# Twelve unread products in front, and another order for the folds and sums of layer 0

## The chip, the cores and the metric

The kernel runs on one core of a Trainium2 chip. The metric is the time of one execution on the device in microseconds (us). Three executions of the kernel before took 771.44, 772.28 and 772.64 us; the median is 772.28.

The engines' names in the profile are PE (TensorE, the matrix products; PEld is its weight load), DVE (VectorE), ACT (ScalarE), POOL (GpSimd) and SP, whose queue issues the loads and stores here. Each runs its own instructions in program order; they wait for one another through semaphores.

## What is computed

Two layers, each a Fourier block and a linear-attention block with residual sums, on x of 2048 rows by 640 columns. Cut to its core:

```python
def _A_ref(x, dft_seq_re, dft_seq_im, dft_hid_re, dft_hid_im):
    a = jnp.einsum("bsd,ed->bse", x, dft_hid_re)
    b = jnp.einsum("bsd,ed->bse", x, dft_hid_im)
    return jnp.einsum("ts,bse->bte", dft_seq_re, a) - jnp.einsum("ts,bse->bte", dft_seq_im, b)

def _B_ref(x, wqkv, wo):                       # 32 heads of 20
    q, k, v = split_heads(x @ wqkv)
    phi = lambda t: jnp.where(t > 0, t + 1, jnp.exp(t)) + 1e-6
    kv = jnp.einsum("bhsd,bhse->bhde", phi(k), v)
    z = phi(k).sum(over s)
    o = (phi(q) @ kv) / (phi(q) . z + 1e-6)
    return merge_heads(o) @ wo

for layer in range(2):
    x = x + _A_ref(_layernorm(x), ...)
    x = x + _B_ref(_layernorm(x), wqkv, wo)
```

## The kernel before

x stands in 16 tiles of 128 rows by 640 columns, x0 to x15. The host permutes rows and columns so that the symmetries of the real Fourier transform become plain sums and differences of tiles. Float32 operands of most products are split into a high and a low part, so that one product of the reference is three on TensorE; the low parts come from subtractions on VectorE (L122, `split`) after a copy on ScalarE (L121).

**The start of layer 0.** The tiles form four quads of four. Per tile there is a fold (the letter `f`, L665, or L663 where it also returns a row sum), a difference (`d`, L670), two columns that have no mirror (`k`, L780), and statistics (`s`: on VectorE L743 to L745, on ScalarE L739 and L740, or a fold's sum with ScalarE's L735). Per quad there are the scales (`r`, `scales2`: L756, L758, L759 on VectorE or POOL, then a power, L760, always on POOL) and the shifts (`o`, L768 and L769, on POOL here). Then follow the normalization (`n`, `norm2`, L776 and L777 on ScalarE), two sums (`a` and `b`, L807; for quad 0 `a` is L803 to L805), and the quad's odd part (`c`, L679, with one more row copied by L681 for quad 0). The odd parts are the moving operands of the first products on TensorE, 20 products of 128 by 512 against the class-2 cosines `cw` (L1010). Their sums are split (`u`, L938 and L939) and feed the hidden transforms (L956). `t`, `z`, `p`, `m` give the even parts, `x` loads a class of cosines, `w` and `v` split the hidden matrices, `R` and `V` swap parts of rows and tiles between the odd parts, and `g` prepares three rows (L1151 and L1152).

The string START lists all of this in the order in which the engines get it: each entry has a letter, the number of a tile or a quad in hexadecimal, and the engine (`v` VectorE, `a` ScalarE, `p` POOL, `d` a load on SP's queue). `Fold.script` (L619) walks through it. There is already a letter for products that nobody reads:

```python
            if kind == "h":
                pw = k.psum()
                for _ in range(int(c or 1)):
                    nc.tensor.matmul(pw[:, :512], k.ident, self.X[i][:, :512], start=True, stop=True)
                continue
```

It opens a PSUM buffer and multiplies the identity with 512 columns of a tile of x.

**The loads.** SP's queue loads the tiles of x in order; LOADS says behind which tiles the four class-2 loads (256 KB each) stand.

**The rest of layer 0.** The Fourier outputs follow a plan (PLANS): `o` an output pair (mixed by L984 to L988 and L995, L996), `s` a sequence product of a class and a column block (L915, L920) whose result is split into `u` by `keep` (L121, L122; class 0 has two columns more, which a second, small split takes), `w` and `q` the weights' splits, `b` and `t` the start of attention with the first statistics (L94 to L96). There are four PSUM buffers of 1024 columns, used in turn, so a sequence product waits until the split of the fourth before it has read its buffer. Keys, values and a Gram matrix follow (L155, L241), then the combine of the heads (L393, L403, L439 and splits of 120 by 120 and 120 by 640), then the outputs: per tile L439 on POOL, a sum over each head's denominators (L455), a reciprocal (L456, L457), a division (L459, L465), transposes on TensorE (L127), a split and products with the weights (L155). Outside the start, a scheduler decides the order of instructions by priorities; AHEAD moves single pieces of work forward or back in it by an offset, keyed by part, name and index (part 0 is layer 0 up to its combine).

**Check and saves.** While keys and values run, VectorE reduces pieces of the constants (L1085, a check of the symmetries); STEPS says at which tiles in the two halves of that loop, in both layers. SAVES says where layer 0 stores its split weights for layer 1. The check's verdict (L1107 to L1119) comes with the first outputs of layer 1.

```python
                if check is not None and n in STEPS[1]:
                    check.step(n != STEPS[1][-1])
```

Of the kernel before, what the change touches and what calls it, by code (L numbers as in the profile page):

```python
# [39 lines left out]
RESID = ((4, 4), (0, 3))  # L40
PLANS = ('o11 s02 s01 s12 s00 s10 s11 b w q o03t', 's00 o12 s10 s11 b s01 s02 s12 o01t w q')
COL = (0, 1, 3, 2)
WLOWS = ((4, 0), (1, 1))
PAUSES = (4, 10, 11, 12, 13, 14)
AHEAD = {'2keep00': -60, '2out10': -600, '1q13': 60, '2keep01': 600, '2keep02': 5, '0kv0': 60, '2out02': -20, '1q14': 60, '2out01': 20, '0kv2': -600, '0m1': -5, '0kv5': 60, '1weigh15': -20, '1res13': 5, '2m1': -20, '0first': -5, '2out12': -200, '2weigh1': 5, '2first': 60, '0m3': 20, '2out13': -200, '0hi01': 200, '0query5': -5, '0chunks9': -20, '0lo10': 60, '0begin': 200, '0norm1': -600, '0lo03': -600, '0key8': -200, '0lo02': -20, '0hi02': 600, '0key1': -20, '0chunks6': -600, '0query7': 20, '0norm10': -600, '0key10': 60, '0stats6': 20, '0w0': 60, '0stats5': -200, '0lo13': -60, '0out02': 600, '0key3': -60, '0norm9': -200, '0pks8': -600, '0stats2': 600, '0hi11': 600, '0lo11': 60, '0pks3': 600, '0query1': 60, '0query2': 5, '0query0': 600, '0normed3': -20, '0out00': -600, '0query10': 200, '0hi03': -60, '0query4': -5, '0out11': -600, '0chunks3': 5, '0normed7': -200, '0out12': -600, '0pks5': -5, '0normed8': -60, '0pks0': 600, '0key2': 600, '0norm3': 60, '0chunks0': 200, '0stats7': 600, '0keep10': 60, '0keep02': 20, '0keep00': -20, '0lo00': 600, '0keep01': -60, '0out03': 600, '0key4': 200, '0chunks4': 60, '0lo12': -200, '0stats9': 200, '0chunks7': -5, '0chunks2': 5, '0norm14': 20, '0wo2': -600, '0gram7': -20, '0stats13': -200, '0pks7': -20, '0normed2': 20, '0stats15': 60, '0gram6': 20, '0pks9': -600, '0stats11': -60, '0norm6': 600, '0key9': 600, '0kv4': -200, '0chunks5': -60, '0chunks13': 60, '0wo0': -20, '0normed13': 20, '0key13': -5, '0normed14': -600, '0pks6': -600, '0chunks15': -600, '0normed0': 200, '0chunks12': -600, '0acc': 20, '0query13': 5, '0chunks11': 20, '0chunks14': -5, '0gram0': 60, '0weigh1': -20, '0pks10': 20, '0key7': 60, '0gram15': 200, '0norm2': -5, '0chunks10': 200, '0pks13': 60, '0query8': 600, '0gram12': -200, '0query15': 5, '0pks14': 5, '0pks2': -5, '0norm11': -600, '0normed10': 60, '0chunks1': -600, '0pks4': 20, '0pks12': 200, '0gram4': -20, '0wo5': -20, '0gram2': -600, '0normed1': 600, '0gram11': 600, '0stats4': -200, '0gram10': -600, '0norm5': -20, '0stats12': -5}


class K:
# [111 lines left out]
class Attention:  # L160
# [92 lines left out]
    def keys_values(self, check=None, keep=1, saves=()):  # L253
# [619 lines left out]
class Fourier:  # L873
# [249 lines left out]
def fast_path(k, ctx, x, wqkv, wo, mask, sign, cls, cex, hid, ckc, ckh, out):  # L1123
# [259 lines left out]
```

## Time and profile before

| | us |
|---|---|
| median of three executions (lowest, highest) | 772.28 (771.44, 772.64) |
| the profiled execution | 772.54 |
| its span in the profile | 770.7 |
| TensorE busy | 734.4 |
| VectorE busy | 571.4 |
| ScalarE busy | 342.8 |
| POOL busy | 251.0 |
| first product on TensorE | 23.05 |

The span runs from the first to the last instruction in the profile. A line of a timeline has the start, the duration, the engine, the line of the kernel, the operation, what it writes and reads, the size and the number of instructions, and in brackets how long the engine had been idle and what ended that. A line of a table of windows has the window and its length, then for PE, PEld, DVE, ACT and POOL the busy time and in brackets the number of instructions, the granted TensorE clock as a share, the DMA engines' busy share, and GB/s. A product of float32 operands leaves two records; a product's records overlap, so that the spacing of their starts is shorter than their duration.

### The profile page before, as it was taken

The numbers are of one execution on the slowest core, as the hardware profiler recorded it, in microseconds if no ns is written. First come the engines' busy times: TensorE is split into PE (matmuls) and PEld (weight loads), VectorE is DVE, ScalarE is ACT, GpSimd is POOL, SyncE is SP. The second block draws the span as 40 slices with busy tenths as digits, with TensorE's granted clock in tenths as the row PEclk, the third lists the DMA queues.
The fourth block names the chain that finished last, engine by engine and source line by source line (L and its number), as shares of the span: only waits on it lengthen the run. The fifth ranks groups of instructions, "written<-read, shape, count | busy, mean of one in ns | idle before, by whom it ended". The sixth has DMA issues, their size and how long they took to land.

```text
span 770.7 us, 12819 instructions
## 1 busy us (share of the span) xinstructions
PE 734.4 (95%) x4862; PEld 703.1 (91%) x4862; DVE 571.4 (74%) x1147; ACT 342.8 (44%) x649; POOL 251.0 (33%) x266
## 2 busy tenths in 40 slices
PE   0899999999999999999999999999999999989996
PEld 0388999999999999899977999999999999979996
DVE  7999865658737697888975794566873799599982
ACT  7744444454334534455682334445433454331110
POOL 5347932220011112467763581111002111143300
PEclk9999999999999999999999999999999999999999
DMA  9222515332716443500052220424231443101112
GB/s 325 92 89 86 160 29 189 114 108 78 250 64 182 147 153 93 155 1 1 19 188 69 69 91 1 148 76 146 58 111 55 146 148 121 52 12 70 69 70 72
DMA packets 35101, 79.13 MB, mean 103 GB/s; under 512 B 4276, under 2 KB 6071, under 8 KB 35031
## 3 DMA queue, kind: packets, MB, share of 16 engines
q1 hardware_dynamic: 35031, 78.23, 32.1%
q8 instruction: 40, 0.66, 0.4%
q14 instruction: 30, 0.25, 0.1%
HBM read 66.01 MB, written 11.80 MB: 101 GB/s over the span
## 4 chain that ended last, share of the span: by engine, by line
PE 74%; DVE 15%; ACT 5%; DMA 2%; issue 1%; POOL 1%; SPq 0%; DVEq 0%; ACTq 0%; POOLq 0%
PE ps L155 46%; PE ps L241 14%; PE ps L956 5%; PE ps L127 4%; PE ps L1010 2%; DVE w L122 2%; PE ps L915 2%; DVE t L122 2%; DMA x<-in_x 2%; DVE t L459 1%; DVE ps L455 1%; DVE x L481 1%; PE ps L393 1%; ACT ab L776 1%; ACT ab L777 1%
## 5 line engine op out<-in xcount | busy, mean ns | idle before, releaser
L155 PE MATMUL ps<-w,t 128*128 128x320 f32 x2880 | 439.0, 311 | 2.0 <-DVE t L122 1.2
L155 PEld LDWEIGHTS ps<-w,t 128*128 128x128 f32 x2880 | 423.1, 188 | 2.8 <-DVE t L122 1.7
L241 PE MATMUL ps<-t,t 128*128 128x256 f32 (+1 forms) x640 | 139.8, 309 | 0.0
L289 POOL TENSOR_TENSOR t<-t,s 128x640 f32<-128x640 f32 x32 | 57.7, 1802 | 222.0 <-DVE s L276 206.9
L273 ACT ACTIVATE t<-ps 128x640 f32<-128x640 f32 x64 | 45.2, 706 | 154.0 <-PE ps L155 154.0
L241 PEld LDWEIGHTS ps<-t,t 128*128 128x128 f32 x640 | 107.4, 188 | 0.0
L1085 DVE CUSTOM_DVE_ANT_0 junk<-ck,ck 128x688 bf16<-128x688 f32 (+5 forms) x138 | 100.0, 724 | 3.2 <-DMA ck<-in_ck 1.3
L241 PE MATMUL ps<-w,t 128*128 128x384 f32 (+1 forms) x320 | 98.7, 310 | 0.3 <-DVE w L122 0.3
L439 POOL TENSOR_TENSOR t<-pq,t 128x640 f32<-128x640 f32 x32 | 53.9, 1690 | 96.4 <-ACT t L362 46.4
L122 DVE TENSOR_TENSOR t<-ps,t 128x640 fp32r<-128x640 f32 (+1 forms) x66 | 53.9, 817 | 40.5 <-ACT t L121 39.7
L121 ACT CAST t<-ps 128x640 fp32r<-128x640 f32 (+1 forms) x66 | 45.8, 694 | 82.7 <-PE ps L127 78.1
L276 DVE SCALAR_TENSOR_TENSOR pq<-t,pq 128x640 f32<-128x640 f32 x32 | 26.8, 837 | 56.5 <-ACT t L275 56.5
L241 PEld LDWEIGHTS ps<-w,t 128*128 128x128 f32 x320 | 60.2, 188 | 0.7 <-DVE w L122 0.5
L1010 PE MATMUL ps<-cw,ab 128*128 128x512 f32 x80 | 37.4, 624 | 23.0 <-DMA cw<-in_se 23.0
L1010 PEld LDWEIGHTS ps<-cw,ab 128*128 128x128 f32 x80 | 15.6, 200 | 42.2 <-ACT ab L777 23.0
L956 PE MATMUL ps<-t,u 128*128 128x322 f32 x306 | 48.0, 315 | 0.2 <-DVE u L939 0.2
L275 ACT ACTIVATE t<-t 128x640 f32<-128x640 f32 x64 | 48.0, 750 | 0.0
L956 PEld LDWEIGHTS ps<-t,u 128*128 128x128 f32 x306 | 45.9, 189 | 1.7 <-ACT u L938 0.8
L127 PE MATMUL ps<-ident,t 128*128 128x128 f32 x320 | 46.1, 275 | 0.1
L122 DVE TENSOR_TENSOR t<-t,t 128x640 fp32r<-128x640 f32 x32 | 26.3, 823 | 20.4 <-ACT t L121 20.3
L115 DVE TENSOR_SCALAR t<-x,kept 128x640 f32<-128x640 f32 x58 | 40.6, 701 | 0.8 <-PE ps L241 0.8
L121 ACT CAST t<-t 128x640 fp32r<-128x640 f32 x32 | 23.3, 729 | 38.7 <-DVE t L115 38.7
(171 smaller groups left out, 885.6 us busy)
## 6 DMA issues: line engine op xcount, KB each, us to landing
ck<-in_ck SPq DMA_DIRECT2D x48, 346.0 KB
ck<-in_ck SPq DMA_DIRECT2D x48, 344.0 KB
save<-w SPq DMA_DIRECT2D x20, 320.0 KB
w<-save SPq DMA_DIRECT2D x20, 320.0 KB
x<-in_x SPq DMA_DIRECT2D x16, 320.0 KB
out<-x SPq DMA_DIRECT2D x15, 320.0 KB
raw<-in_wqkv SPq DMA_DIRECT2D x10, 320.0 KB
s<-in_wqkv SPq DMA_DIRECT2D x10, 320.0 KB
```

Of the source, the lines that this page charges most:

```text
L121: self.nc.scalar.copy(hi, src)
L122: self.engine(pool).tensor_tensor(lo, src, hi.bitcast(F32), op=ALU.subtract)
L127: self.nc.tensor.transpose(tp[:, 128 * c : 128 * c + 128], src[:, 128 * c : 128 * c + 128], self.ident)
L155: nc.tensor.matmul(pu[:m, 512 * h : 512 * h + HD], s, w[:, HD * h : HD * h + HD], start=first, stop=last)
L241: nc.tensor.matmul(self.place(G, c, part), x[:, 128 * c : 128 * c + 128], p[:, f : f + n], start=start and i == 0, stop=stop and i == 2, s ...
L273: nc.scalar.activation(h2(e), halves(pu), AF.Relu, scale=-1.0)
L275: nc.scalar.activation(e, e, AF.Exp, scale=-1.0)
L289: nc.gpsimd.tensor_tensor(pksum, pksum, pk, op=ALU.add)
L439: k.nc.gpsimd.tensor_tensor(t1, self.PQ[self.order2[n]], self.zb, op=ALU.mult)
L956: self.k.nc.tensor.matmul(po[:, o : o + 322], s[:, f : f + 128], w[:, x, :], start=start, stop=stop)
L1010: self.k.nc.tensor.matmul(self.sum(j), T.out["o", q][:, 128 * j : 128 * j + 128], self.C[2, g], start=n == 0, stop=n == 3)
L1085: i = nc.vector.tensor_tensor_reduce(k.junk[:, : a.shape[1]], b, a, 1.0, 0.0, op0, op1, o)
```

## The change

START gets an entry `h712e` right after its first one: twelve products of the identity with x7, read by nobody, ahead of everything else on TensorE. The rest of START is a new order: quad 0's scale is now computed on POOL whole (`r0p` for `r0v o0p`), POOL takes other folds (`d4p`, `f3p`, `d7p`, `fap` in place of `d4p`, `d3p`, `f3p`, `d7p`, `f8p`, `fap`), and VectorE's and ScalarE's entries stand in another sequence. LOADS puts the first class-2 load behind x12 and the other three behind x14 (before: x9, x13, x15, x15). PLANS of layer 0 moves the sequence product s11 ahead of s00 and s10, and the split of the first weights behind the others. STEPS and SAVES have other tiles, and AHEAD other keys and offsets for part 0; those of the other parts are the same.

```diff
-STEPS = ((2, 3, 5, 6, 7, 10, 11, 12, 13), (0, 3, 7, 10, 14))
-SAVES = ((1, 2, 3, 5, 11), (4, 5, 6, 7, 8))
+STEPS = ((1, 3, 4, 5, 6, 10, 11, 12, 13), (1, 4, 8, 9, 10))
+SAVES = ((1, 2, 4, 8, 9), (0, 1, 5, 6, 8))
-START = 'O0p d0v s0a k1a f0v k2a d1v f1v k0a f2v s1q x00d d2v d4p s3v s2v s4a d3p k6a r0v s5a f6v s6q k3a k5a o0p f3p f7v d7p s7a f8p
...
+START = 'O0p h712e d0v s0a k1a d4p f0v d1v k2a f1v d2v f2v k0a s1q s2v s4a s3v d3v f6v x10d k6a s5a r0p k3a f3p f7v s7a k5a n2a s6q d7p fap f8v
...
-LOADS = (9, 13, 15, 15)
+LOADS = (12, 14, 14, 14)
-PLANS = ('o11 s02 s01 s12 s00 s10 s11 b w q o03t', 's00 o12 s10 s11 b s01 s02 s12 o01t w q')
+PLANS = ('o11 s02 s01 s12 s11 s00 s10 w q b o03t', 's00 o12 s10 s11 b s01 s02 s12 o01t w q')
...
```

On TensorE the twelve products come first; the 20 products with the odd parts follow in the order that they had. How instructions move on VectorE is shown at the three places that the prediction speaks of (ab_8 to ab_23 are the working copies of x0 to x15; the last number of a name is that of its buffer).

First, VectorE in the start, from the folds ahead of quad 3's variances (qve_52 before, qve_53 now) to quad 2's second sum (L807 into ab_16). Before:

```order
L665 TENSOR_TENSOR ab_19_166<-x11_120 128x319
L670 TENSOR_TENSOR ab_20_167<-x12_122 128x319
L670 TENSOR_TENSOR ab_21_168<-x13_124 128x319
L665 TENSOR_TENSOR ab_17_164<-x9_114 128x319
L756 TENSOR_SCALAR qve_52_325<-qmv_42_258 128x3
L758 TENSOR_SCALAR qve_52_325<-qmv_42_258 128x1
L759 TENSOR_SCALAR qmv_42_258<-qmv_42_258 128x1
L670 TENSOR_TENSOR ab_19_166<-x11_120 128x319
L670 TENSOR_TENSOR ab_16_163<-x8_112 128x319
L807 SCALAR_TENSOR_TENSOR ab_17_164<-ab_17_164,qrs_48_277,ab_18_165 128x640
L665 TENSOR_TENSOR ab_23_170<-x15_130 128x319
L807 SCALAR_TENSOR_TENSOR ab_16_163<-ab_16_163,qrs_48_277,ab_19_166 128x640
```

Now:

```order
L670 TENSOR_TENSOR ab_20_167<-x12_120 128x319
L670 TENSOR_TENSOR ab_21_168<-x13_124 128x319
L756 TENSOR_SCALAR qve_53_335<-qmv_42_263 128x3
L758 TENSOR_SCALAR qve_53_335<-qmv_42_263 128x1
L759 TENSOR_SCALAR qmv_42_263<-qmv_42_263 128x1
L670 TENSOR_TENSOR ab_17_164<-x9_114 128x319
L670 TENSOR_TENSOR ab_16_163<-x8_112 128x319
L665 TENSOR_TENSOR ab_17_164<-x9_114 128x319
L670 TENSOR_TENSOR ab_19_166<-x11_118 128x319
L665 TENSOR_TENSOR ab_23_170<-x15_134 128x319
L807 SCALAR_TENSOR_TENSOR ab_17_164<-ab_17_164,qrs_49_291,ab_18_165 128x640
L807 SCALAR_TENSOR_TENSOR ab_16_163<-ab_16_163,qrs_49_291,ab_19_166 128x640
```

From quad 1's odd part (L679 into ab_14, row not shown) to the variances there were five folds and differences, of which four stand here, and there are three now, of which two stand here. Behind the variances five of them stand in a row ahead of the first L807, where there were two, and the two L807 follow each other.

Second, VectorE in the Fourier outputs of layer 0, from the split of the first sequence product's sums (u_119 before, u_120 now, 128x2x256) to the small split of the same product's two further columns (128x2), after which its PSUM buffer is free. Before:

```order
L122 TENSOR_TENSOR u_119_599<-ps_117_592,u_118_598 128x2x256
L96 BN_AGGR kept_195_880<-st_197_882 128x2
L94 BN_STATS st_223_1074<-x15_130 128x6
L95 BN_STATS st_223_1074<-x15_130 128x6
L95 BN_STATS st_210_977<-x12_122 128x6
L987 TENSOR_TENSOR x13_124<-x13_124,t_115_583 128x321
L122 TENSOR_TENSOR u_122_613<-ps_120_606,u_121_612 128x2x256
L94 BN_STATS st_240_1185<-x9_114 128x6
L122 TENSOR_TENSOR u_119_599<-ps_117_592,u_118_598 128x2
```

Now:

```order
L122 TENSOR_TENSOR u_120_612<-ps_118_605,u_119_611 128x2x256
L96 BN_AGGR kept_167_735<-st_169_737 128x2
L96 BN_AGGR kept_196_893<-st_198_895 128x2
L987 TENSOR_TENSOR x13_124<-x13_124,t_116_596 128x321
L95 BN_STATS st_211_990<-x12_120 128x6
L122 TENSOR_TENSOR u_123_626<-ps_121_619,u_122_625 128x2x256
L94 BN_STATS st_228_1101<-x15_134 128x6
L95 BN_STATS st_228_1101<-x15_134 128x6
L122 TENSOR_TENSOR u_120_612<-ps_118_605,u_119_611 128x2
```

One half of a tile's statistics (L94 or L95) fewer stands ahead of the small split, three in place of four, and one aggregate (L96) more. L1152, which stood among the first mixes (L984), now stands ahead of the first of them.

Third, VectorE where the outputs of layer 1 begin. Before:

```order
L457 RECIPROCAL rden_1254_7490<-den_1253_7489 128x32
L122 TENSOR_TENSOR w_1243_7448<-ps_1241_7440,w_1242_7447 120x640
L122 TENSOR_TENSOR w_1246_7461<-ps_1244_7453,w_1245_7460 120x640
L456 TENSOR_SCALAR den_1262_7570<-den_1262_7570 128x32
L459 TENSOR_TENSOR t_1250_7479<-pq_1126_6774,rden_1254_7490 128x5x120
L122 TENSOR_TENSOR w_1249_7474<-ps_1247_7466,w_1248_7473 120x640
L465 TENSOR_TENSOR t_1250_7479<-pq_1126_6774,rden_1254_7490 128x2x5x4
L122 TENSOR_TENSOR t_1259_7557<-ps_1252_7483,t_1258_7556 128x640
L457 RECIPROCAL rden_1263_7571<-den_1262_7570 128x32
L455 TENSOR_REDUCE den_1269_7622<-t_1260_7562 128x32
L1109 TENSOR_REDUCE cktop_7544<-ps_1256_7542 8x1
```

Now:

```order
L122 TENSOR_TENSOR w_1244_7461<-ps_1242_7453,w_1243_7460 120x640
L122 TENSOR_TENSOR w_1247_7474<-ps_1245_7466,w_1246_7473 120x640
L455 TENSOR_REDUCE den_1263_7583<-t_1252_7494 128x32
L456 TENSOR_SCALAR den_1254_7502<-den_1254_7502 128x32
L122 TENSOR_TENSOR w_1250_7487<-ps_1248_7479,w_1249_7486 120x640
L122 TENSOR_TENSOR t_1260_7570<-ps_1253_7496,t_1259_7569 128x640
L456 TENSOR_SCALAR den_1263_7583<-den_1263_7583 128x32
L457 RECIPROCAL rden_1255_7503<-den_1254_7502 128x32
L1109 TENSOR_REDUCE cktop_7557<-ps_1257_7555 8x1
L457 RECIPROCAL rden_1264_7584<-den_1263_7583 128x32
L459 TENSOR_TENSOR t_1251_7492<-pq_1131_6803,rden_1255_7503 128x5x120
```

The last weight split (w_1249 before, w_1250 now), the split of the first tile's transposed rows (t_1259, now t_1260) and the check's maximum (L1109) stood behind the first of these divisions (L459), and stand ahead of it now.

More of the change, by code (lines that the diff above doesn't have):

```diff
@@ L30 @@
 CUT = 10
-STEPS = ((2, 3, 5, 6, 7, 10, 11, 12, 13), (0, 3, 7, 10, 14))
-SAVES = ((1, 2, 3, 5, 11), (4, 5, 6, 7, 8))
-START = 'O0p d0v s0a k1a f0v k2a d1v f1v k0a f2v s1q x00d d2v d4p s3v s2v s4a d3p k6a r0v s5a f6v s6q k3a k5a o0p f3p f7v d7p s7a f8p s8v s9v n2a k4a sav d6v x10d dav n3a fap n0a kaa sda r1v kfa o1p sbv b0v k7a f4v r2v sev a0v sca d5v n7a c0v dfv f5v n6a a1v b1v dev c1v d9v o2p sfa fbv R0a dcv k8a ddv f9v r3v dbv k9a x01d w01a naa d8v b2v kba V0a x11d nba ffv o3p w00a a2v fev kca c2v fcv kda kea fdv nfa a3v w02a nea b3v c3v t2v v01v V1a t3v v00v t0v t1v w12a v02v u23v w10a u21v u20v u22v w11a v11v v10v u24v v12v z0v p0v p1v m1p m0v g0a'
+STEPS = ((1, 3, 4, 5, 6, 10, 11, 12, 13), (1, 4, 8, 9, 10))
+SAVES = ((1, 2, 4, 8, 9), (0, 1, 5, 6, 8))
+START = 'O0p h712e d0v s0a k1a d4p f0v d1v k2a f1v d2v f2v k0a s1q s2v s4a s3v d3v f6v x10d k6a s5a r0p k3a f3p f7v s7a k5a n2a s6q d7p fap f8v s9v n3a s8v sav sca n0a d6v sda dav d5v x00d r1v kaa k7a b0v kfa k4a sbv f4v r2v sev o1p a0v n7a dfv c0v f5v a1v n6a b1v dev c1v sfa R0a fbv dcv ddv o2p r3v d9v d8v f9v dbv k8a x01d k9a naa w01a kba nba ffv V0a b2v a2v fev x11d c2v kca o3p fcv fdv kea nfa w02a kda w00a a3v nea b3v c3v V1a v00v v01v t3v v02v t1v t0v w11a t2v u23v w10a u21v u20v u24v w12a v11v u22v v12v v10v g0a z0v p0v m0v p1v m1p'
 SECOND = 'x02d x12d x22d x32d x00d x01d x10d x11d W00d W01d W02d W10d | w00a | w01a v00v W11d | w02a v01v W12d | v02v | R0a V0a w10a | O0p sfa v10v ffv dfp kfa r3p | w11a c2v v11v w12a nfa v12v nea t2p a3v b3v c3v V1a t3p p1v m1p u20v u21v u23v u24v u22v'
@@ L44 @@
 PAUSES = (4, 10, 11, 12, 13, 14)
-AHEAD = {'2keep00': -60, '2out10': -600, '1q13': 60, '2keep01': 600, '2keep02': 5, '0kv0': 60, '2out02': -20, '1q14': 60, '2out01': 20, '0kv2': -600, '0m1': -5, '0kv5': 60, '1weigh15': -20, '1res13': 5, '2m1': -20, '0first': -5, '2out12': -200, '2weigh1': 5, '2first': 60, '0m3': 20, '2out13': -200, '0hi01': 200, '0query5': -5, '0chunks9': -20, '0lo10': 60, '0begin': 200, '0norm1': -600, '0lo03': -600, '0key8': -200, '0lo02': -20, '0hi02': 600, '0key1': -20, '0chunks6': -600, '0query7': 20, '0norm10': -600, '0key10': 60, '0stats6': 20, '0w0': 60, '0stats5': -200, '0lo13': -60, '0out02': 600, '0key3': -60, '0norm9': -200, '0pks8': -600, '0stats2': 600, '0hi11': 600, '0lo11': 60, '0pks3': 600, '0query1': 60, '0query2': 5, '0query0': 600, '0normed3': -20, '0out00': -600, '0query10': 200, '0hi03': -60, '0query4': -5, '0out11': -600, '0chunks3': 5, '0normed7': -200, '0out12': -600, '0pks5': -5, '0normed8': -60, '0pks0': 600, '0key2': 600, '0norm3': 60, '0chunks0': 200, '0stats7': 600, '0keep10': 60, '0keep02': 20, '0keep00': -20, '0lo00': 600, '0keep01': -60, '0out03': 600, '0key4': 200, '0chunks4': 60, '0lo12': -200, '0stats9': 200, '0chunks7': -5, '0chunks2': 5, '0norm14': 20, '0wo2': -600, '0gram7': -20, '0stats13': -200, '0pks7': -20, '0normed2': 20, '0stats15': 60, '0gram6': 20, '0pks9': -600, '0stats11': -60, '0norm6': 600, '0key9': 600, '0kv4': -200, '0chunks5': -60, '0chunks13': 60, '0wo0': -20, '0normed13': 20, '0key13': -5, '0normed14': -600, '0pks6': -600, '0chunks15': -600, '0normed0': 200, '0chunks12': -600, '0acc': 20, '0query13': 5, '0chunks11': 20, '0chunks14': -5, '0gram0': 60, '0weigh1': -20, '0pks10': 20, '0key7': 60, '0gram15': 200, '0norm2': -5, '0chunks10': 200, '0pks13': 60, '0query8': 600, '0gram12': -200, '0query15': 5, '0pks14': 5, '0pks2': -5, '0norm11': -600, '0normed10': 60, '0chunks1': -600, '0pks4': 20, '0pks12': 200, '0gram4': -20, '0wo5': -20, '0gram2': -600, '0normed1': 600, '0gram11': 600, '0stats4': -200, '0gram10': -600, '0norm5': -20, '0stats12': -5}
@@ new lines @@
+AHEAD = {'2keep00': -60, '2out10': -600, '1q13': 60, '2keep01': 600, '2keep02': 5, '0kv0': -5, '2out02': -20, '1q14': 60, '2out01': 20, '0kv2': 5, '0m1': -5, '0kv5': 200, '1weigh15': -20, '1res13': 5, '2m1': -20, '0first': -5, '2out12': -200, '2weigh1': 5, '2first': 60, '2out13': -200, '0hi01': 200, '0chunks9': 600, '0lo10': -200, '0lo03': -600, '0lo02': 20, '0key1': -5, '0norm10': -600, '0key10': 600, '0stats6': 20, '0w0': 60, '0lo13': -60, '0out02': 600, '0key3': 20, '0pks8': -5, '0stats2': 20, '0hi11': 200, '0lo11': 60, '0query0': -200, '0normed3': 60, '0out00': -600, '0out11': -600, '0chunks3': -600, '0out12': -600, '0pks0': 200, '0keep10': 60, '0keep02': 20, '0lo00': 600, '0keep01': -60, '0out03': 600, '0key4': -60, '0chunks4': 20, '0lo12': -60, '0chunks7': -20, '0chunks2': 5, '0gram7': -600, '0normed2': -60, '0stats15': 60, '0gram6': -200, '0kv4': -5, '0chunks5': 5, '0chunks13': 60, '0wo0': -20, '0normed13': 20, '0chunks15': -600, '0normed0': -60, '0chunks11': 60, '0gram15': 200, '0norm2': -5, '0chunks10': 200, '0gram12': 20, '0query15': 5, '0pks2': -5, '0chunks1': -600, '0wo5': 5, '0gram2': -5, '0normed1': 600, '0gram11': 600, '0gram8': -200, '0normed4': 5, '0key12': 20, '0stats3': -20, '0pks15': -20, '0stats0': -600, '0query6': -60, '0gram3': 200, '0norm12': 200, '0query3': 5, '0gram9': -20, '0gram1': 60, '0norm15': -20, '0chunks8': 200, '0weigh1': 60, '0stats8': -200, '0hi00': -5, '0pks14': 200, '0hi13': 5, '0m2': 200, '0kv1': -200, '0query13': 600, '0norm8': -200, '0norm13': 600, '0gram13': -5, '0norm5': -200, '0gram5': -60, '0out10': -20, '0pks9': -60, '0norm11': -200, '0pz2': -600, '0stats1': 20, '0norm3': -20, '0norm9': -20, '0keep00': 600, '0gram10': -200, '0normed8': -200, '0pks5': 5, '0m5': 20, '0norm7': -600, '0key6': 600, '0query1': 60, '0query2': -20, '0normed5': 60, '0pks6': -20, '0stats7': -600, '0norm0': 60, '0key14': 5, '0weigh0': 20, '0m0': -60, '0query14': -60, '0normed9': 60, '0key8': -5, '0pks10': -600, '0chunks0': 600, '0pz0': -60, '0query12': -5, '0stats12': 200, '0query4': -600, '0stats11': -20, '0zb': -5, '0stats5': 20, '0query10': 5}
```

## The prediction

> **What bounds the kernel now.** I read the page first, then the engines' timelines where TensorE stops.
>
> ```profile
> span 770.7 us, 12819 instructions
> PE 734.4 (95%) x4862; PEld 703.1 (91%) x4862; DVE 571.4 (74%) x1147; ACT 342.8 (44%) x649; POOL 251.0 (33%) x266
> PE   0899999999999999999999999999999999989996
> PE 74%; DVE 15%; ACT 5%; DMA 2%; issue 1%; POOL 1%; SPq 0%; DVEq 0%; ACTq 0%; POOLq 0%
> ```
>
> TensorE is busy in every slice but the first and the last, and the change adds and removes none of its products but twelve in front. So time can come only from the start, from the few places where TensorE waits, and from its clock. What lies between (the layers' long streams of products) moves earlier or later as a block. The start comes first; the columns are start, duration, engine, line.
>
> ```profile
> 23.05 3.75 PE L1010 MATMUL ps<-cw,ab 128*128 128x512 f32 x4 [23.05 <-DMA cw<-in_se]
> 27.53 4.03 PE L1010 MATMUL ps<-cw,ab 128*128 128x512 f32 x9
> 42.82 0.42 PE L956 MATMUL ps<-t,u 128*128 128x322 f32 x1
> L1010 PE MATMUL ps<-cw,ab x40: 592/592/1194, 23.0 to 42.2; 128*128 128x512 f32 x40
> 22.63 0.32 DVE L681 COPY ab<-t 1x321 f32<-1x321 f32 x1
> 25.67 0.80 DVE L679 TENSOR_TENSOR ab<-ab,ab 128x640 f32<-128x640 f32 x1
> 36.45 0.82 DVE L679 TENSOR_TENSOR ab<-ab,ab 128x640 f32<-128x640 f32 x1
> ```
>
> The 20 products of L1010 leave 40 records, two each. The first four stand (3.75 - 1.19) / 3 = 0.85 us apart, those from 27.53 on (4.03 - 0.59) / 8 = 0.43 us: TensorE begins at half speed. Program order gives 4 records to the odd part of quad 0 (ready 22.95), 16 to that of quad 1 (ready 26.47), 8 to quad 2's, and 12 to quad 3's (ready 37.27). From 37.27 to L956 at 42.82 are 5.5 us, 12 records of 0.46. So two ready times, 26.47 and 37.27, set the end of this stage, not the clock alone.
>
> **The twelve products.** They need x7 and the identity.
>
> ```profile
> 10.91 0.48 DVE L665 TENSOR_TENSOR ab<-x 128x319 f32<-128x319 f32 x1
> ```
>
> This is x7's first reader, and x7's place in the load queue does not change: the new products start near 10.95. They are 24 records. With one stretch of half speed as long as the later one below shows (3.4 us), and up to as long again before it begins, full speed comes between 14.4 and 17.8: 4 to 8 records at 0.85, 16 to 20 at 0.43, end 22.9 to 24.6. L1010's first four follow by 24.6 to 26.3, still before quad 1's part at 26.47, so up to there nothing is lost or won: that wait is the cover. After it, the half-speed records from 26.59 to 27.53 took 0.94 where 0.43 would do: 0.5 us is won there, and from quad 1 on 36 records of 0.43 to 0.46 end at 42.0 to 43.0. But quad 3's part gates the last twelve: with 37.27 unchanged the win is nearly nothing. The new order puts two folds fewer ahead of quad 3's variances (L756 to L759); two folds are 2 x 0.40 by the starts of consecutive ones. Between 0 and 0.6 us I take **0.3**.
>
> [...]
>
> **What the new order risks in the start.** POOL computes each quad's scale (L760).
>
> ```profile
> 18.77 1.01 POOL L760 TENSOR_TENSOR qrs<-qve,mhalf 128x4 f32<-128x4 f32 x1
> 28.60 0.87 DVE L670 TENSOR_TENSOR ab<-x 128x319 f32<-128x319 f32 x2
> 28.69 2.85 POOL L760 TENSOR_TENSOR qrs<-qve,mhalf 128x4 f32<-128x4 f32 x1 [7.56 <-DVE qmv L759]
> 30.83 0.89 DVE L807 SCALAR_TENSOR_TENSOR ab<-ab,qrs,ab 128x640 f32<-128x640 f32 x1 [0.17 <-ACT ab L777]
> 31.61 0.56 POOL L768 TENSOR_TENSOR qmv<-qmv,qrs 128x4 f32<-128x4 f32 x1
> 31.63 0.48 DVE L665 TENSOR_TENSOR ab<-x 128x319 f32<-128x319 f32 x1
> 32.03 0.82 DVE L679 TENSOR_TENSOR ab<-ab,ab 128x640 f32<-128x640 f32 x1
> 11.96 0.19 POOL L769 TENSOR_TENSOR qbo<-qmv 128x2 f32<-128x2 f32 x1
> 32.25 0.65 POOL L769 TENSOR_TENSOR qbo<-qmv 128x2 f32<-128x2 f32 x1
> 32.94 0.66 ACT L776 ACTIVATE ab<-ab,qbo,qrs 128x321 f32<-128x321 f32 x1 [1.40 <-POOL qbo L769]
> ```
>
> Quad 3's scale took 2.85 us, where 1.01 is usual. VectorE ran folds and sums of two SBUF inputs without a break until 30.83 - 0.17 = 30.66, where it waited for ScalarE; the scale ended at 31.54, 0.88 later. So it seems to have stood still until that gap. The shift (L769, 0.19 alone) took 0.65 and ended with L679 at 32.9, ScalarE waited 1.40 for it, and quad 3's part came at 37.27, 6.6 us after the gap. [...]
>
> L768 did end at 32.17, between L665's end at 32.11 and that of L679, so a small POOL operation can get in without a gap, and the rows don't settle it. The forecast takes no longer stop than before.
>
> The rest of the start (folds that change engine between VectorE and POOL, quad 0's whole scale on POOL, class-2 loads behind x12 and x14) lies under the wait for quad 0's part: TensorE reads the first class-2 load after 22.95, and x15, which now comes behind all four of these loads, is needed only for quad 3. Without that cover each fold would cost its 0.40 and each load its place in the queue.
>
> **The wait at 63.08.** In the first half of the Fourier outputs, a sequence product waits for a PSUM buffer.
>
> ```profile
> 50.98 0.49 DVE L984 TENSOR_TENSOR t<-ps,t 128x322 f32<-128x322 f32 x1 [0.97 <-ACT t L981]
> 53.34 0.47 DVE L1152 TENSOR_TENSOR cx<-t,cx 1x258 fp32r<-1x258 f32 x1
> 59.55 0.67 DVE L122 TENSOR_TENSOR u<-ps,u 128x512 fp32r<-128x512 f32 x1
> 60.62 0.86 DVE L95 BATCH_NORM_STATS2 st<-x 128x6 f32<-128x320 f32 x2
> 62.40 0.48 DVE L94 BATCH_NORM_STATS2 st<-x 128x6 f32<-128x320 f32 x1
> 62.80 0.13 DVE L122 TENSOR_TENSOR u<-ps,u 128x2 fp32r<-128x2 f32 x1
> 63.08 3.69 PE L915 MATMUL ps<-cw,ab 128*128 128x256 f32 x16 [1.22 <-DVE u L122]
> ```
>
> The two-column split at 62.80 frees the buffer; VectorE is behind, with no break around it (3.42 of 3.42 us in the last row of the next fence). In the new order one half-tile statistic fewer (0.40) stands ahead of it, and L1152 (some 0.4 of its 0.47, since neighbours overlap) moves ahead of the first L984, into VectorE's wait of 0.97. So the buffer comes 0.8 us sooner; TensorE's 1.22 falls to 0.4. Bounds: 0, if VectorE is late by as much elsewhere, and 1.22. I take **0.8**. What follows on TensorE up to the combine stands at 9 in the page's slices, so it moves as a block and gives nothing back.
>
> **Layer 0's combine.**
>
> ```profile
> 312.25 0.55 PE L155 MATMUL ps<-w,w 120*120 120x320 f32 x2 [1.00 <-DVE w L122]
> 313.18 2.73 PE L155 MATMUL ps<-w,w 120*120 120x320 f32 x12 [0.38 <-DVE t L122]
> 311.20:314.20 3.00, 1.63 (x10) 1.31 (x10) 3.00 (x5) 1.39 (x2) 2.41 (x2) 1.00 0.17 30
> 314.20:317.60 3.40, 3.40 (x16) 3.36 (x15) 2.67 (x4) 1.97 (x3) 0.00 (x0) 0.50 0.17 33
> 61.62:65.04 3.42, 2.20 (x11) 1.78 (x10) 3.42 (x12) 0.84 (x3) 3.42 (x8) 1.00 0.00 0
> ```
>
> The last two waits, 1.38 us together, are followed by 3.4 us at clock 0.50, worth 1.7 us. The order of VectorE, ScalarE, POOL and TensorE there is unchanged; only the first two weight splits come sooner, and they are early already. These waits stay: 0.
>
> **Layer 1's combine** (the check's steps move here too).
>
> ```profile
> 685.26 3.20 PE L155 MATMUL ps<-w,t 128*128 128x320 f32 x20 [0.79 <-DVE w L122]
> 690.89 0.17 PE L1111 MATMUL ps<-ident,cktop 8*1 8x8 f32 x1 [0.85 <-DVE cktop L1109]
> 685.90 1.60 POOL L439 TENSOR_TENSOR t<-pq,t 128x640 f32<-128x640 f32 x1 [3.18 <-DMA w<-t]
> 685.94 2.20 DVE L459 TENSOR_TENSOR t<-pq,rden 128x600 f32<-128x600 f32 x1
> 688.06 0.81 DVE L122 TENSOR_TENSOR w<-ps,w 120x640 fp32r<-120x640 f32 x1
> ```
>
> Now one reduction (L455) in place of two stands ahead of the weight splits for which 685.26 waits, and the last weight split (688.06), the first tile's split and the check's maximum (L1109) come ahead of the second tile's division (L459), which takes 2.20 here, beside POOL. That can free TensorE of 0.79 + 0.85 = 1.6 us. But the division, which the second tile's transposes need, comes later by two splits of 0.81 and the maximum, some 1.7 us; its cover is the first tile's ten products, 1.7 us, and without that the loss is as long. From a gain of 1.6 to a loss of 1.5, I take a gain of **0.5**: the two waits are on TensorE for certain, the cover is just long enough.
>
> **Sum.** The profiled execution took 772.54 us (span 770.7 and 1.8 around it): 772.54 - 0.3 - 0.8 - 0.5 = 770.94. It lies 0.26 above the median of the runs shown, 772.28, so the forecast against that median is **770.7 us**.
>
> **The rivals.**
> First, the scale of quad 3 starves. In the new order eleven two-input operations of VectorE follow its variances, and the sum of quad 2 that had the gap ahead of it closes it if ScalarE is 0.2 us sooner. The eleven take 8 x 0.40 + 2 x 0.80 + 0.74 = 5.5 us from 28.1 on: the scale would get in at 33.6 instead of 30.66, and with the same 6.6 us behind it quad 3's part comes at 40.2, 2.9 us late; 2.0 if L768 and L769 then lose no 0.46 each. For it: the 2.85 row. Against: L768's entry. It decides once the gap comes after 31.0. The price stands in place of the 0.3: 770.7 + 0.3 + 2.0 to 2.9 is 773.0 to 773.9, slower than before.
> Second, the half-clock stretch at 314 goes: 770.7 - 1.7 = 769.0. For it: all work there comes 1.1 us sooner, and a wait of 1.22 inside one such length (the row at 61.62) drew no half clock, so 1.38 is a near thing. Against: the waits stay. [...]
> Third, layer 1's combine loses 1.5 instead of gaining 0.5: 772.7. For it: the divisions that come later meet POOL's products; against: TensorE's products of the first tile run meanwhile.
> Fourth, the new products do nothing and x7 is late: TensorE's first used product then starts after 23.5, worth under 0.5, part of the forecast's width.
>
> **Chances.** Forecast 0.46 (769.8 to 771.6), starving scale 0.20, half clock gone 0.22, combine worse 0.12. A measurement here tells 0.2%, 1.54 us, from no change: below 770.74 is faster, above 773.82 slower. Faster: 0.6 of the forecast, nearly all of the second rival, together 0.50. Slower: nearly half of the first rival, a third of the third, 0.13. Same: 0.37. The range 768.4 to 773.8 holds all four but their tails and the dearer half of the first rival.
>
> **What would show it.** Right: quad 3's part before 37.3 and L956 starting by 42.6; the wait at 63 under 0.6; L1111 without a wait. Wrong: an L760 of over 3 us near 28 and L956 after 44; a wait of over 1 us for transposes near 690; a clock of 0.50 in other places than before.

## The result and the profile after

The change made the kernel slower: 773.73 us (median of 19 executions, 771.34 to 775.43) against 771.07 us (19 executions of the kernel before beside them, 769.70 to 773.63). The ratio is 1.0032, with a 95% interval of 1.0022 to 1.0042. The forecast was 770.7 us, faster by a little.

The page of the changed kernel: its span, the busy times, TensorE's slices, and the shares of the chain that ended last.

```profile
span 773.3 us, 12864 instructions
PE 747.2 (97%) x4886; PEld 708.9 (92%) x4886; DVE 575.1 (74%) x1146; ACT 342.9 (44%) x649; POOL 256.2 (33%) x267
PE   4899999999999999999999999999999999999997
PE 76%; DVE 15%; ACT 3%; POOL 2%; issue 2%; DMA 1%; SPq 1%; DVEq 0%; ACTq 0%; POOLq 0%
```

The span grew by 2.6 us and TensorE's busy time by 12.8, nearly all of it the unread products' own 13.2. POOL's share of the chain, 1% before, is 2%. The timelines of TensorE, POOL, ScalarE and VectorE in the start of the changed kernel show why:

```profile
11.21 13.19 PE L633 MATMUL ps<-x,ident 128*128 128x512 f32 x24 [11.21 <-DMA x<-in_x]
24.24 1.88 PE L1010 MATMUL ps<-cw,ab 128*128 128x512 f32 x4
26.85 10.54 PE L1010 MATMUL ps<-cw,ab 128*128 128x512 f32 x24 [0.73 <-issue]
40.16 7.09 PE L1010 MATMUL ps<-cw,ab 128*128 128x512 f32 x12 [2.78 <-DVE ab L679]
46.69 11.50 PE L956 MATMUL ps<-t,u 128*128 128x322 f32 x72
28.16 6.38 POOL L760 TENSOR_TENSOR qrs<-qve,mhalf 128x4 f32<-128x4 f32 x1 [4.83 <-DVE qmv L759]
35.13 0.66 ACT L776 ACTIVATE ab<-ab,qbo,qrs 128x321 f32<-128x321 f32 x1 [3.73 <-POOL qbo L769]
32.80 0.87 DVE L665 TENSOR_TENSOR ab<-x 128x319 f32<-128x319 f32 x2
36.33 0.88 DVE L807 SCALAR_TENSOR_TENSOR ab<-ab,qrs,ab 128x640 f32<-128x640 f32 x1 [2.65 <-ACT ab L777]
39.19 0.82 DVE L679 TENSOR_TENSOR ab<-ab,ab 128x640 f32<-128x640 f32 x1
```

And the chain that ended last, in order of time (start, length, engine, tile, line):

```profile
28.16 6.39 POOL qrs L760
```

Quad 3's scale took 6.38 us (2.85 before). VectorE's run of folds and sums ended at 33.67, and the scale 0.87 later, at 34.54. ScalarE waited 3.73 us for the shift, quad 3's odd part came at 40.01 instead of 37.27, and TensorE, at full speed by then, stood 2.78 us. L956 starts 3.87 us later than before. Of these, 2.74 are quad 3's delay; the rest is the clock, in a table of windows (the column behind the five engines is the granted clock):

```profile
37.40:40.20 2.80, 0.04 (x1) 0.07 (x1) 1.89 (x3) 1.07 (x4) 0.00 (x0) 1.00 0.00 0
40.50:43.80 3.30, 3.30 (x5) 1.35 (x4) 3.30 (x6) 0.50 (x2) 0.00 (x0) 0.50 0.56 137
43.90:46.70 2.80, 2.80 (x9) 1.15 (x7) 1.60 (x3) 1.93 (x4) 0.00 (x0) 1.00 0.22 86
```

After the wait TensorE ran 3.4 us at half speed, so that the last twelve records took 6.5 us (40.16 to 46.69) instead of 5.4 (42.65 - 37.24 in the run with the products alone, e2 below). That adds 1.1 us. The two rows of e2:

```profile
37.24 5.39 PE L1010 MATMUL ps<-cw,ab 128*128 128x512 f32 x12 [0.31 <-DVE ab L679]
42.65 0.56 PE L956 MATMUL ps<-t,u 128*128 128x322 f32 x2
```

The other places of the prediction, in TensorE's timeline after:

```profile
65.54 1.54 PE L915 MATMUL ps<-cw,ab 128*128 128x258 f32 x6 [0.19 <-DVE u L122]
315.41 0.55 PE L155 MATMUL ps<-w,w 120*120 120x320 f32 x2 [0.99 <-DVE w L122]
687.78 2.90 PE L155 MATMUL ps<-w,t 128*128 128x320 f32 x18 [0.20 <-DVE w L122]
692.56 0.17 PE L1111 MATMUL ps<-ident,cktop 8*1 8x8 f32 x1
693.71 0.74 PE L127 MATMUL ps<-ident,t 128*128 128x128 f32 x5 [0.99 <-DVE t L465]
```

The wait of 1.22 at 63 is 0.19. The same wait of the first combine stands at 315.41 (312.25 before): 3.16 us late, so 0.71 of the 3.87 were won back up to there. In the second combine the waits of 0.79 and 0.85 are 0.20 and none, but a wait of 0.99 for the second tile's division is new. The transposes that waited there began at 690.99 before:

```profile
690.99 0.76 PE L127 MATMUL ps<-ident,t 128*128 128x128 f32 x5
```

They are 2.72 us late, so 0.44 more was won back, and 2.6 remain in the span.

### The profile page after: what moved, and what is told of

It reads as the page before. It is cut to its first block, busy times and chain, and to the rows that moved or that the text cites. A ratio compares the mean times of both kernels' runs of the same rounds, so it can differ in the third digit from the quotient of the medians.

```text
span 773.3 us, 12864 instructions
## 1 busy us (share of the span) xinstructions
PE 747.2 (97%) x4886; PEld 708.9 (92%) x4886; DVE 575.1 (74%) x1146; ACT 342.9 (44%) x649; POOL 256.2 (33%) x267
## 4 chain that ended last, share of the span: by engine, by line
PE 76%; DVE 15%; ACT 3%; POOL 2%; issue 2%; DMA 1%; SPq 1%; DVEq 0%; ACTq 0%; POOLq 0%
PE ps L155 47%; PE ps L241 17%; PE ps L127 3%; PE ps L1010 3%; PE ps L956 2%; PE ps L393 2%; DVE t L122 1%; DVE w L122 1%; PE ps L915 1%; DMA x<-in_x 1%; DVE ps L455 1%; DVE x L481 1%; POOL qrs L760 1%; DVE t L459 1%; DVE st L95 1%
## 5 line engine op out<-in xcount | busy, mean ns | idle before, releaser
L956 PE MATMUL ps<-t,u 128*128 128x322 f32 x306 | 48.4, 316 | 0.2 <-DVE t L122 0.2
L956 PEld LDWEIGHTS ps<-t,u 128*128 128x128 f32 x306 | 45.9, 189 | 1.6 <-DVE u L939 0.5
L115 DVE TENSOR_SCALAR t<-x,kept 128x640 f32<-128x640 f32 x58 | 42.3, 729 | 3.1 <-PE ps L241 3.1
L127 PEld LDWEIGHTS ps<-ident,t 128*128 128x128 f32 x320 | 38.7, 142 | 2.7 <-POOL t L439 1.1
```

The lines of the kernel that those rows point to most:

```text
L127: self.nc.tensor.transpose(tp[:, 128 * c : 128 * c + 128], src[:, 128 * c : 128 * c + 128], self.ident)
L956: self.k.nc.tensor.matmul(po[:, o : o + 322], s[:, f : f + 128], w[:, x, :], start=start, stop=stop)
```

## The experiments

All times are medians; each ratio is to the kernel before, run beside it on the same chip (its median was 772.50 us beside e1 to e8 and 771.43 beside e9 to e11), so kernels are compared by their ratios. The last three columns come from the one profiled execution of each kernel. "Quad 3" is the end of its L679, "L956" the start of its first product in the profile.

| run | us | ratio (95% interval) | L760 | quad 3 | L956 |
|---|---|---|---|---|---|
| before | 771.07 | 1 | 2.85 | 37.27 | 42.82 |
| the change | 773.73 | 1.0032 (1.0022 to 1.0042) | 6.38 | 40.01 | 46.69 |
| e1 no products | 772.94 | 1.0007 (0.9991 to 1.0022) | 6.38 | 40.07 | 45.63 |
| e2 products alone | 772.94 | 1.0008 (0.9992 to 1.0024) | 2.85 | 37.09 | 42.65 |
| e3 two statistics | 774.07 | 1.0021 (1.0005 to 1.0037) | 1.01 | 39.60 | 46.16 |
| e4 two folds, with a wait | 769.68 | 0.9962 (0.9946 to 0.9978) | 1.25 | 36.87 | 42.42 |
| e5 two folds, no wait | 775.49 | 1.0037 (1.0023 to 1.0051) | 7.18 | 40.87 | 46.42 |
| e6 tiny gap | 769.18 | 0.9956 (0.9942 to 0.9970) | 1.25 | 35.70 | 41.44 |
| e7 rest alone | 772.16 | 0.9995 (0.9985 to 1.0005) | 2.85 | 37.03 | 42.68 |
| e8 as e4, no products | 769.49 | 0.9950 (0.9937 to 0.9964) | 1.25 | 36.52 | 43.04 |
| e9 before, gap closed | 773.26 | 1.0026 (1.0014 to 1.0038) | 5.98 | 39.44 | 44.99 |
| e10 before, products and gap | 770.50 | 0.9989 (0.9974 to 1.0005) | 1.25 | 35.61 | 41.22 |
| e11 tiny gap, no products | 769.11 | 0.9965 (0.9952 to 0.9979) | 1.25 | 35.86 | 42.61 |

**Are the products to blame?** The change without them, and they alone in the kernel before:

```diff
-START = 'O0p h712e d0v s0a ...
+START = 'O0p d0v s0a ...
```

> The changed kernel without the twelve unread products (h712e left out of START), all else as changed. Theory: POOL's scale of quad 3 (L760, 6.38 us from 28.16) stands still while VectorE runs operations of two SBUF inputs without a break; the products have no part in it. Then L760 again takes over 6 us, quad 3's odd part comes near 40, L956 starts at 45 to 47, and the time is 773 to 774.5 us. Rival: the products are what costs (they hold TensorE until 24.4 and shift its clock): then L956 starts by 43 and the time falls to 770 to 771.

> The kernel before with only the twelve unread products in front (h712e into its START). Theory: L760 keeps its 2.85 us, TensorE is at full speed from 17 on, L956 starts at 42.2 to 42.8, and the time is 0 to 1 us under that of before, 770.0 to 771.0. Rival (the products cost): L956 after 44 and a time over 772.5.

L760 stayed at 6.38 us without the products and at 2.85 with them alone: they have no part in POOL's delay, and L956 moved as the theory said. The times were less clear than expected. Alone the products change nothing that can be measured. In the changed kernel, leaving them out brought the ratio from 1.0032 to 1.0007, and the intervals of the two only touch. The expected 773 to 774.5 us were missed by more than the 772.94 suggests, for the kernel before took 772.50 beside it: 0.4 us more than before, where 2 to 3 were expected. The profile of e1 shows a way for that: without the products TensorE reached quad 3's part later, waited 1.54 us instead of 2.78, and kept its clock (granted 1.00 from 40.2 to 45.6).

```profile
40.22 5.39 PE L1010 MATMUL ps<-cw,ab 128*128 128x512 f32 x12 [1.54 <-DVE ab L679]
45.63 0.57 PE L956 MATMUL ps<-t,u 128*128 128x322 f32 x2
```

**What lets POOL in?** For this the walk through START got a letter `j`, work on VectorE that nobody reads, put behind quad 3's variances:

```diff
+            if kind == "j": [nc.vector.bn_stats(k.small([128, 2, 6], "st")[:, 0, :], self.X[i][:, :HD]) if e == "v" else nc.vector.memset(self.junk[:, :1], 0.0) if e == "m" else nc.vector.tensor_tensor(self.junk[:, 1:HD] if e == "t" or not _ else self.junk[:, HC:], self.X[i][:, 1:HD], self.X[i][:, HC:], op=ALU.add) for _ in range(int(c))]; continue
-START = '... o2p r3v d9v d8v f9v ...
+START = '... o2p r3v jf2v d9v d8v f9v ...      e3: two bn_stats of x15, one SBUF input each
+START = '... o2p r3v jf2t d9v d8v f9v ...      e4: two folds of x15 into the same half of a junk tile
+START = '... o2p r3v jf2w d9v d8v f9v ...      e5: two folds of x15 into its two halves
+START = '... o2p r3v d9v jf2m d8v f9v ...      e6: two memsets of one column of the junk tile
```

> The changed kernel with two statistics of one SBUF input each (bn_stats of x15, read by nobody, 0.8 us together) on VectorE right behind quad 3's variances. Theory: POOL's scale gets in while they run, L760 takes under 1.9 us, quad 3's odd part comes by 38, L956 starts by 43.5, TensorE's clock shows no half-speed stretch near 40, and the time falls by 2 to 4 us to 770 to 771.5 although VectorE has more to do. Rival (POOL waits for something else, such as its operands or its own sequencer): more work on VectorE, so L760 stays over 6 us and the time is 773.5 to 775.

> The same place and the same 0.8 us, but two folds (L665's form, two SBUF inputs, into a junk tile) in place of the two statistics. Theory: they don't let POOL in, L760 takes about 7.2 us, quad 3's odd part comes near 40.8, L956 starts after 46.5, and the time is 773.5 to 775. Rival (any 0.8 us between the variances and the next fold would do, since POOL only needs time): as with the two statistics, 770 to 771.5.

Both came out against their numbers. POOL's timeline in e3:

```profile
28.05 1.01 POOL L760 TENSOR_TENSOR qrs<-qve,mhalf 128x4 f32<-128x4 f32 x1 [4.83 <-DVE qmv L759]
29.13 5.28 POOL L768 TENSOR_TENSOR qmv<-qmv,qrs 128x4 f32<-128x4 f32 x1
34.49 0.20 POOL L769 TENSOR_TENSOR qbo<-qmv 128x2 f32<-128x2 f32 x1
```

VectorE's timeline in e4, the two folds:

```profile
27.89 1.00 DVE L629 TENSOR_TENSOR t<-x 128x319 f32<-128x319 f32 x2
```

And POOL's in e4:

```profile
27.98 1.25 POOL L760 TENSOR_TENSOR qrs<-qve,mhalf 128x4 f32<-128x4 f32 x1 [4.83 <-DVE qmv L759]
29.31 0.44 POOL L768 TENSOR_TENSOR qmv<-qmv,qrs 128x4 f32<-128x4 f32 x1
```

In e3 the scale did run freely beside the one-input statistics, in 1.01 us, as the theory had it. But the next POOL operation, L768 (0.20 alone), fell into the run of two-input operations behind them and took 5.28: the delay had only moved one instruction on. In e4 the two folds should have kept POOL out and did not. They write the same columns, so the second waits for the first: the pair takes 1.00 us where two folds in a row take 0.87. The theory was therefore narrowed to the gap between two operations, and e5 takes only that wait away.

> As in the run with two folds behind the variances, but the second fold writes the other half of the junk tile, so that it doesn't wait for the first. Theory, mended: POOL gets in at a real gap between two VectorE operations, however short (the second fold's wait for the first made one of 34 ns at 28.36); VectorE operations that overlap their neighbour by 71 ns keep POOL out for as long as they follow each other. Then without the wait L760 takes about 7.2 us, L956 starts after 46.5, and the time is 773.5 to 775.5 us. Rival (0.8 us of folds is enough): L760 1.25, L956 by 42.5, 769 to 770.5.

The two folds in VectorE's timeline in e5:

```profile
28.14 0.87 DVE L629 TENSOR_TENSOR t<-x 128x319 f32<-128x319 f32 x2
```

And the scale in POOL's:

```profile
28.23 7.18 POOL L760 TENSOR_TENSOR qrs<-qve,mhalf 128x4 f32<-128x4 f32 x1 [4.83 <-DVE qmv L759]
```

The same work without the wait gives 7.18 us, the 6.38 of the change and the 0.8 that the run is longer. Last, a gap with next to no work:

> The changed kernel with two memsets of one column of the junk tile on VectorE behind the first fold after quad 3's variances; the second waits for the first. Theory: the gap alone, with nearly no work, lets POOL in: L760 under 1.8 us, quad 3's odd part by 36.0, L956 at 42.4, and 768.5 to 770.5 us. Rival (POOL needs time as well as a gap): L760 over 5 us and 773 to 775.

VectorE's timeline in e6:

```profile
27.52 0.47 DVE L670 TENSOR_TENSOR ab<-x 128x319 f32<-128x319 f32 x1
27.94 0.06 DVE L629 MEMSET t<- 128x1 f32 x1
28.05 0.48 DVE L670 TENSOR_TENSOR ab<-x 128x319 f32<-128x319 f32 x1
28.07 0.06 DVE L629 MEMSET t<- 128x1 f32 x1
28.45 0.48 DVE L665 TENSOR_TENSOR ab<-x 128x319 f32<-128x319 f32 x1
```

POOL's in e6:

```profile
27.61 1.25 POOL L760 TENSOR_TENSOR qrs<-qve,mhalf 128x4 f32<-128x4 f32 x1 [4.83 <-DVE qmv L759]
28.94 0.45 POOL L768 TENSOR_TENSOR qmv<-qmv,qrs 128x4 f32<-128x4 f32 x1
29.47 0.32 POOL L769 TENSOR_TENSOR qbo<-qmv 128x2 f32<-128x2 f32 x1
```

And TensorE's in e6:

```profile
26.30 15.69 PE L1010 MATMUL ps<-cw,ab 128*128 128x512 f32 x36 [0.77 <-issue]
41.44 3.76 PE L956 MATMUL ps<-t,u 128*128 128x322 f32 x20
```

The first memset ends at 28.00 and the next operation with two inputs starts at 28.05 (the second memset stands beside it, at 28.07); elsewhere such an operation starts 0.07 to 0.08 us before its neighbour ends (28.05 + 0.48 against 28.45). That break of 0.05 us was enough. A memset reads nothing, so e6 alone doesn't tell the gap from an operation without SBUF inputs in the row; e4 against e5, folds in both, does. Here L760 took 1.25 us, TensorE's 36 records from quad 1 on ran without a wait, and L956 started at 41.44. The time, 0.9956 of before, beats both kernels.

**Does the kernel before live by such a gap?** It had one, 0.17 us at 30.66. One fold more, without a wait, ahead of the sum that waited there:

```diff
-... nba ffv o3p w00a a2v ...
+... nba ffv jf1w o3p w00a a2v ...
```

> The kernel before with one fold more (0.4 us, two SBUF inputs, into a junk tile, no wait) on VectorE ahead of quad 2's second sum, the one that waited 0.17 us for ScalarE at 30.66. Theory: this closes the only gap in the run, so the kernel before falls into the same state as the changed one: L760 takes over 5 us (2.85 before), quad 3's odd part comes near 40, L956 starts at 45 to 46, and the time rises by 2 to 3 us, ratio 1.002 to 1.004. Rival (something else in the new order holds POOL): L760 at most 3.3 us, L956 within 0.5 us of before, ratio 0.999 to 1.001.

VectorE's timeline at that place:

```profile
30.45 0.47 DVE L629 TENSOR_TENSOR t<-x 128x319 f32<-128x319 f32 x1
30.85 0.87 DVE L807 SCALAR_TENSOR_TENSOR ab<-ab,qrs,ab 128x640 f32<-128x640 f32 x1
```

And POOL's:

```profile
28.54 5.98 POOL L760 TENSOR_TENSOR qrs<-qve,mhalf 128x4 f32<-128x4 f32 x1 [7.56 <-DVE qmv L759]
```

The sum starts at 30.85 instead of 30.83, with no wait ahead of it: VectorE lost next to nothing there, and yet the kernel before became 0.26% slower (0.14 to 0.38), all but as slow as the changed one.

**What are the other parts worth?** The change with START and LOADS of the kernel before:

```diff
-START = 'O0p h712e d0v s0a k1a d4p ...
-LOADS = (12, 14, 14, 14)
+START = 'O0p d0v s0a k1a f0v k2a ...
+LOADS = (9, 13, 15, 15)
```

> The changed kernel with START and LOADS of the kernel before (no unread products, folds and loads in their old order), so only STEPS, SAVES, the plan of layer 0 and the priorities are new. Theory: these are worth what TensorE's waits at 63 and in layer 1's combine lost less in the changed kernel, 0.5 to 1.1 and 0.6 to 1.5 us: 1.1 to 2.2 us under the kernel before, ratio 0.997 to 0.9986. Rival (that gain hung on the new start): ratio 0.999 to 1.001.

The mended starts of e4 and e6 without the products (e8 and e11):

```diff
-START = 'O0p h712e d0v ...
+START = 'O0p d0v ...
```

> The two folds with the wait between them, and without the twelve unread products. Theory: with quad 3's part at 36 the sums from quad 1 on are TensorE's bound, so half speed after 23.5 costs: L956 0.3 to 1.5 us later than with the products (42.42), time 769.8 to 771.2. Rival (products cost or do nothing): same as with them or less, 769.0 to 769.8.

> The changed kernel with the two memsets of one column behind the first fold after quad 3's variances, and without the twelve unread products. Theory: L760 at 1.3 us as with them; TensorE starts at half speed near 23.2, which with quad 3's part early costs 0.5 to 1.5 us against 41.4 at L956 (with the products); ratio 0.996 to 0.9975. Rival (the products are worth nothing in the time): ratio 0.9945 to 0.996.

And the kernel before with products and gap:

```diff
-START = 'O0p d0v ... f9v r3v dbv k9a ...
+START = 'O0p h712e d0v ... f9v r3v dbv jf2m k9a ...
```

> The kernel before with the twelve unread products and the two memsets of one column behind the first difference after quad 3's variances. Theory: L760 falls from 2.85 to 1.3 us, quad 3's odd part comes near 36, TensorE is at full speed and never waits for it, L956 starts near 41.5 to 42 (42.82 before), and the time is 0.8 to 1.3 us under before, ratio 0.998 to 0.999. Rival (the old order wins as much as the new one once the gap is there): ratio 0.995 to 0.997.

With quad 3's part early, L956 starts 0.6 us (e4, e8) and 1.2 us (e6, e11) sooner with the products, as expected, but the ratios don't show it: 0.9962 against 0.9950, and 0.9956 against 0.9965, within their intervals (e8's time is its rival's, e11's ratio the expected one). STEPS, SAVES, the plan and the priorities alone give nothing (e7), against the expectation. TensorE's timeline there:

```profile
62.35 1.54 PE L915 MATMUL ps<-cw,ab 128*128 128x258 f32 x6 [0.98 <-DVE u L122]
76.51 1.74 PE L956 MATMUL ps<-t,u 128*128 128x322 f32 x10 [0.95 <-DVE t L122]
```

The wait at 63 stays at 0.98 and another of 0.95 is new: the new plan and priorities don't win that place without the new start. The new start without them was not run. With the old order, gap and products won 0.11%, which can't be told from nothing (e10, 0.9974 to 1.0005), though L956 started 1.6 us sooner. A little of it went at the clock: of e10's 12 executions six had a mean granted clock of 0.998 or more, and their median is 769.77 us; of the kernel before beside them 17 of 25 had it, with 770.86. So at the same clock 1.1 us arrived. Where the other 0.5 went is open.

## Why the prediction was wrong

**The step that failed** is the choice "The forecast takes no longer stop than before" in the start, and the term of 0.3 us gained. The prediction's first rival is what happened. It was priced at 2.0 to 2.9 us; the profile shows 2.74 at quad 3's part. It was given 0.20, because L768 had seemed to get in without a gap (32.17 in the kernel before). e3 shows that it does not where POOL hasn't been let in at a gap shortly before: there L768 stood for 5.28 us. The run's length was the better measure: 6.38 in the change, 7.18 with two folds more (e5), and 5.98 in the kernel before with its gap closed (e9).

**What the price lacked** was the clock. The prediction treated a wait of TensorE as its length. Here the products brought TensorE to quad 3's products early and at full speed, so that it stood 2.78 us and then ran 3.4 us at half speed, 1.1 us more. So the products, "0.5 us is won there", made the result worse in this order, as the ratios of the change and of e1 say, 1.0032 and 1.0007. That they do it through the clock is read from the two profiles, and the mean granted clock, on record for every execution, agrees. In the 13 profiles a mean of 0.998 or more goes with no stretch of half speed between the first full speed and the last product, 0.996 and 0.997 with one, 0.994 with two. The medians by this clock, in us, with the number of executions (times compare within a row only, since the change was taken beside other executions of the kernel before):

| | 0.998 or more | 0.995 to 0.997 | 0.994 or less |
|---|---|---|---|
| before, beside e1 to e4 | 771.66 (26) | 773.80 (9) | none |
| the change | 772.51 (5) | 773.21 (6) | 774.97 (8) |
| e1 no products | 771.66 (4) | 773.07 (8) | none |

With the products and POOL kept out (the change, e3, e5), 18 of 36 executions lie at 0.994 or less; without the products (e1, e9), none of 24 does.

**The bound on the products** held: quad 3's part gates the last twelve records. With the products alone L956 came 0.17 us sooner (e2), no more than quad 3's part itself, 0.18 sooner in that profile. They ran from 11.21 to 24.4, near what was worked out, and full speed came inside them: in the change their records stand 0.85 us apart from 11.21 on and 0.43 from 16.46 on.

```profile
11.21 3.75 PE L633 MATMUL ps<-x,ident 128*128 128x512 f32 x4 [11.21 <-DMA x<-in_x]
16.46 4.07 PE L633 MATMUL ps<-x,ident 128*128 128x512 f32 x9
```

That half speed lasts there for a stretch of 3.4 us and "up to as long again before it begins" was an estimate; no run shows the second term as such, and the change shows 5.25 us in all (16.46 - 11.21).

**The wait at 63** was right in the profile: 0.8 forecast, 1.22 - 0.19 = 1.03 at the wait itself and 0.71 up to the combine. But its reason, that the plan and one statistic fewer do it, was not the whole of it, since they don't do it without the new start (e7).

**Layer 0's combine** stayed as forecast in the profile, its wait of 0.99 and the half speed behind it included; that half speed is not there in every execution (see the end). **Layer 1's combine** won 0.4 us where 0.5 was forecast, in the way weighed there: two waits less, and one of 0.99 for the later division.

So the terms were 0.3, 0.8 and 0.5 gained, and the measured ones 3.87 lost, 0.71 and 0.44 gained: 2.7 lost, beside 2.6 in the span. The range held 773.73, but the side was wrong. That the first rival's 773.0 to 773.9 us hold it too is luck: against the 772.28 from which they were worked out they are 0.7 to 1.6 more, and 2.7 more were measured, against 771.07, with the clock's 1.1 among them.

e3 points to VectorE's two SBUF inputs as what keeps POOL out: the scale took 1.01 us beside one-input statistics, and L768 5.28 beside two-input folds. To wait for the end of one VectorE instruction would have cost at most 0.9 us (an estimate, from the 0.89 that L807 took in the kernel before); the runs show that POOL is kept out over the whole run of overlapping instructions, eleven of them in the change, where the scale took 6.38 us.

## What to carry to other kernels

Where a POOL operation like L760 is on the critical path, issue it into a stretch where VectorE has a real gap (a wait on its own last result was enough: with 0.05 us in e6, L760 took 1.25 us instead of 6.38) or runs operations of one SBUF input for as long as POOL's chain takes (in e3 L760 took 1.01 us, but the next POOL operation was caught, for 5.28). A VectorE order without idle time can be slower than one that waits a few hundredths of a microsecond in the right place (1.0032 of before for the change, 0.9956 for e6), and when an edit closes VectorE's gaps, ask which POOL operation lived on them (L760 went from 2.85 to 5.98 us in e9). A wait of TensorE may cost more than its length, because the clock can fall behind it (the change: 2.78 us, then 3.4 us at 0.50, 1.1 us more), the more so if an edit brings TensorE to it sooner (e1, without the products: 1.54 us, and the clock stayed at 1.00).

## What the runs showed of the hardware

- After POOL has been let in at a gap, its next operations get in too, with no further gap in VectorE's rows: L768 took 0.45 and L769 0.32 us in e6, while VectorE's folds took 0.48 instead of 0.47. After one-input operations it was not so (e3, L768 5.28 us). Why is open.
- Half speed does not follow from the length of a wait alone. In the profile of e5 TensorE stood 3.51 us and kept its clock, where in the change 2.78 us drew 3.4 us of half speed. That execution of e5 is the exception: its mean clock is 0.999 and its time 773.15 us, the other four have 0.992 to 0.994 and 774.72 to 776.78. The wait of e5, and the windows of the wait and of the time behind it, columns as above:

```profile
41.02 5.39 PE L1010 MATMUL ps<-cw,ab 128*128 128x512 f32 x12 [3.51 <-DVE ab L679]
37.60:41.00 3.40, 0.00 (x0) 0.01 (x1) 2.30 (x4) 1.67 (x6) 0.00 (x0) 1.00 0.00 0
41.00:44.40 3.40, 3.38 (x8) 1.62 (x9) 3.40 (x7) 1.35 (x5) 0.00 (x0) 1.00 0.50 130
```

- The same waits in layer 0's combine (0.99 and 0.37 us) drew half speed in the change and none in e6. The window behind them in the change, and in e6 a window from inside the first wait (which ends at 310.08) on:

```profile
317.00:320.30 3.30, 3.30 (x16) 3.26 (x15) 2.41 (x5) 1.39 (x2) 0.19 (x1) 0.50 0.17 30
```

```profile
310.00:314.00 4.00, 3.55 (x23) 3.27 (x24) 4.00 (x8) 2.32 (x4) 1.56 (x1) 1.00 0.15 28
```

By its length such a stretch is worth some 1.7 us (an estimate, half of 3.4). At this place it came in 5 of the 13 profiles (before, the change, e1, e4, e10). Such stretches, here and in the start, go with a large part of the spread of some 4 us between the executions of one kernel: the groups of the table above, by clock, lie 2.1 us apart for the kernel before (771.66 and 773.80) and 2.5 for the change (772.51 and 774.97). Why the same waits draw half speed in one execution and not in another is open.
